# Seven-product block multiplication: products over four accumulator banks, batches in alternation, one result tile for two units

## The chip, the cores and the metric

One core of a Trainium2 chip runs the kernel. The metric is device time in microseconds (us) of one execution; three timed executions of the kernel before gave 1161.13, 1161.44 and 1161.69 us. TensorE is called PE, VectorE DVE, ScalarE ACT, GpSimd POOL, SyncE SP (it issues the DMAs).

## What is computed

Attention with a forgetting bias over 4 batches of 576 tokens, then two feed-forward layers on every token. The attention is as in the kernel's first third and is not touched. The layers are:

```python
h = x @ w_in                      # 2304x512 @ 512x2048
g = where(h >= 1, h, where(h <= -1, 0, (h + 1)**2 / 4))
x = g @ w_out                     # 2048x512
a = x @ w_a;  b = x @ w_b         # 512x1536 each
out = (a * b) @ w_out2            # 1536x512
```

## The kernel before

All data lies transposed: 128 features on the partitions, a batch's S = 576 tokens along the row. A *unit* is 128 features of a layer's hidden width: 16 in layer 1, 12 in layer 2. Each number is held as a high and a low part, and a product of two such numbers is three matmuls (`PASSES`, L953). A matmul here has 128 rows, 128 columns of weights and HN = 288 tokens (half a batch).

`ROUNDS` (L28) lists the work: batches 0 and 1 in the plain way, with attention of the other batches among it; then, from about 672 us, batches 2 and 3 through both layers by a seven-product scheme. For two units, the 2x2 block product (two halves of the features, two halves of the tokens) is made of seven products in place of eight. The sums of weight blocks are prepared by `load_set` (tiles `set`, three of them), those of the token blocks by `make_forms` (tiles `form`), once for a batch and layer.

`seven` (L1084) issues the seven products of one pair of units. Each is six matmuls, 288 columns wide. They accumulate in three places: X and Y, the two banks of a pair tile `pp`, and Z, one bank `ps`. The places take intermediate sums: a place is read out and then written on. The order of targets is X, Y, Z, X, Y, X, X (L1094). `gather` (L1123) reads after each of the first six: ACT copies products 0, 1 and 3 into a tile `tmp` (L1135), DVE adds products 2, 4 and 5 to it (L1137). The last X is read by the users: `h_seven` (L1145, relu, square, max/min in pieces of 576 and 288) or `ab_seven` (L1173, the product of a and b). `split_g` makes high and low parts into `g` tiles (L373, L1009). `y_step` (L1190) multiplies the `g` of a block of units by the second weights (matmuls L963) and adds the result to `y` (DVE, L1218; the first block is copied by ACT). In layer 1 a block is four units, in layer 2 two, and a block is finished for one batch before the other's begins.

PSUM has eight banks: two pairs `pp` and four single `ps`. A `product` takes a pair or two singles.

Nothing is placed by hand: each operation enters `Plan` (L140) with an engine, an estimated duration (`act`, `tt`, L272 to L277), a key (its wished time) and what it reads and writes. `Plan.run` then sets out, engine by engine, whatever can start first, and adds `LAT` (L143) after each operation. Each engine runs its list in that order, so the estimates decide the order of the instructions, not their time on the chip. `Banks.find` (L113) hands out PSUM, `Room.find` (L84) the SBUF places: `tmp_room` six tiles of 576 columns (three of them only in the second part), `g_room` seven.

Of the kernel before, what the change touches and what calls it, by code (L numbers as in the profile page):

```python
# [14 lines left out]
ALU = mybir.AluOpType  # L15
# [18 lines left out]
    (2, (2, 3), 0, 12, 2, True),  # L34
# [4 lines left out]

QK32 = 8  # L40
# [4 lines left out]
TMPS = 3  # L45
TMPS_LATE = 3
# [93 lines left out]
class Plan:  # L140


    LAT = {"PE": 0.3, "DVE": 0.2, "ACT": 0.15, "POOL": 0.5, "SP": 0.1}  # L143
# [128 lines left out]
def act(n):  # L272
    return 0.10 + 0.00083 * n


def tt(n):
    return 0.075 + 0.00104 * n  # L277
# [11 lines left out]
def tile_forgetting_attention_two_ffn(  # L289
# [92 lines left out]
    def dma(key, o, i, size, reads, writes, name, q=SP, issue=0.36, lat=2.0):  # L382
# [36 lines left out]
    tmp_room = plan.room(  # L419
        TMPS + TMPS_LATE,  # L420
        lambda k, ref: (const if k < TMPS else pool_of("sets")).tile([P, S], F32, tag=f"tmp{k}", name=f"tmp{k}", bufs=1),
        lambda k: k < TMPS or x_over(k),
    )
# [531 lines left out]
    def product(key, terms, hold, name):  # L955

        ps = bank(key, "either")
        for a in range(2):

            def mm(e, a=a):  # L960
                for k, (w, x, _) in enumerate(terms):
                    for t, (wu, xu) in enumerate(PASSES):
                        nc.tensor.matmul(  # L963
                            bank_of(ps, a)[:, :HN],
                            w(wu),
                            x(xu)[:, a * HN : (a + 1) * HN],
                            start=(k == 0 and t == 0),
                            stop=(k == len(terms) - 1 and t == len(PASSES) - 1),
                        )

            op({PE: 3 * len(terms) * HN * PE1}, key, mm, [r for t in terms for r in t[2]], [(ps, a)], hold=hold, name=name)
        return ps
# [111 lines left out]
    def seven(key, st, b, layer, hold, name, take):  # L1084

        xy, z = bank(key, "pair"), bank(key, "one")

        def at(n):
            return z.t[:, :HN] if n == 2 else xy.t[:, n, :HN]

        def mark(n):
            return (z, 0) if n == 2 else (xy, n)

        for n, (to, w, x, fresh) in enumerate((  # L1094
            (0, A11, B11, True),
            (1, S1, T1, True),
            (2, A12, B21, True),
            (0, S2, T2, False),
            (1, S4, B22, False),
            (0, S3, T3, False),  # L1100
            (0, A22, T4, False),
# [14 lines left out]
            kn = key + 1.6 * n  # L1116
            op({PE: 3 * NG2 * HN * PE1}, kn, mm, need, [mark(to)], hold=hold, name=name)
            take(n, kn - 6, lambda to=to: at(to), mark(to))
        return lambda: at(0), mark(0)

    HALF = (slice(0, HN), slice(HN, S))

    def gather(c):  # L1123

        def take(n, k, src, rd):
            what = {0: (0, 0), 1: (1, 1), 2: (0, 0), 3: (0, 1), 4: (0, 1), 5: (1, 1)}.get(n)
            if what is None:
                return
            f, a = what

            def part():
                return c[f].t[:, HALF[a]]

            if n in (0, 1, 3):
                op({ACT: act(HN)}, k, lambda e: nc.scalar.copy(part(), src()), [rd], [(c[f], a)], name="part")  # L1135
            else:
                op({DVE: tt(HN)}, k, lambda e: nc.vector.tensor_tensor(part(), src(), part(), op=ALU.add),  # L1137
                   [rd], [(c[f], a)], name="partadd")

        return take  # L1140

    def both(t):
        return [(t, 0), (t, 1)]

    def h_seven(key, st, b, g):  # L1145
# [5 lines left out]
        def relu(o, i):  # L1151
            return lambda e: nc.scalar.activation(o(), i(), AF.Relu, bias=0.5, scale=0.5)
# [4 lines left out]
        def at(r, sl):  # L1157
            return lambda: r.t[:, sl]
# [182 lines left out]
```

## Time and profile before

| | before |
|---|---|
| median of 3 runs | 1161.44 us |
| profiled execution, its own time | 1161.19 us |
| its span, first to last instruction | 1159.5 us |
| PE busy | 1078.6 us (93%), 8068 matmuls recorded |
| DVE busy | 734.3 us (63%) |
| ACT busy | 616.8 us (53%) |
| mean granted PE clock | 0.981 |

Busy time of PE counts overlapping matmuls once, with modelled ends; a stretch's matmul count times the distance between starts says more than its busy share. The chain of waits gives PE 74% of the span, ACT 12%, DVE 6%, DMA 5%. "L1106" is line 1106 of the kernel, `pp<-form,set` means a matmul that reads `form` and `set` and writes `pp`.

### The profile page before, as it was taken

What the parts mean: (1) busy time and instruction counts of PE and PEld (TensorE: products, weight loads), DVE (VectorE), ACT (ScalarE), POOL (GpSimd) and SP (SyncE); (2) the same over time, 40 slices, a digit from 0 to 9 for tenths busy, and PEclk for the clock granted to TensorE, in tenths of its full rate; (3) what the DMA queues carried; (4) which work ended last, traced back from release to release, by engine and by line L of the source; (5) the groups of instructions that cost most, each with busy time, mean ns of one, the idle gap of its engine ahead of it and who ended that gap; (6) DMA issues with size and microseconds to landing.
All of it is one profiled execution on the core that took longest, in us unless ns stands there. A gap on an engine that the chain in (4) does not pass through costs nothing.

```text
span 1159.5 us, 20668 instructions
## 1 busy us (share of the span) xinstructions
PE 1078.6 (93%) x8068; PEld 1011.9 (87%) x8068; DVE 734.3 (63%) x1463; ACT 616.8 (53%) x1381; POOL 40.2 (3%) x64
## 2 busy tenths in 40 slices
PE   9998987999999999899999888888888989999998
PEld 5777877998999999899999888888887978899898
DVE  7886673377687856668565574555556745665555
ACT  5986883466797767667653244544445333222211
POOL 2131210000000000000000000000000000000000
PEclk9998997999999999999999899999999899999999
DMA  5766786456475765655363571213131132222012
GB/s 182 229 190 168 178 172 175 153 197 160 171 192 163 198 146 183 165 153 207 91 160 116 174 262 37 108 38 106 41 99 48 38 109 73 96 87 73 3 36 82
DMA packets 84770, 152.35 MB, mean 131 GB/s; under 512 B 21320, under 2 KB 45896, under 8 KB 84672
## 3 DMA queue, kind: packets, MB, share of 16 engines
q1 hardware_dynamic: 84576, 150.88, 43.7%
q8 instruction: 63, 1.03, 0.4%
q14 instruction: 35, 0.29, 0.1%
q10 hardware_dynamic: 96, 0.15, 0.0%
HBM read 107.64 MB, written 42.79 MB: 130 GB/s over the span
## 4 chain that ended last, share of the span: by engine, by line
PE 74%; ACT 12%; DVE 6%; DMA 5%; issue 2%; SPq 0%; POOL 0%; DVEq 0%; ACTq 0%
PE pp L963 43%; PE pp L1106 16%; PE ps L750 3%; PE ps L700 2%; ACT tmp L1135 2%; DMA qkraw<-in_qk 2%; PE ps L1106 2%; PE ps L641 2%; DVE tmp L1137 2%; DMA conv<-in_w_in 2%; ACT p L675 2%; PE ps L963 1%; DMA conv<-in_w_out 1%; ACT pt L373 1%; PE ps L632 1%
## 5 line engine op out<-in xcount | busy, mean ns | idle before, releaser
L963 PE MATMUL pp<-g,whl 128*128 128x288 f32 x2574 | 359.3, 297 | 5.9 <-DVE y L1218 5.9
L963 PEld LDWEIGHTS pp<-g,whl 128*128 128x128 f32 x2574 | 348.7, 190 | 8.1 <-DVE y L1218 7.5
L963 PE MATMUL pp<-x,whl 128*128 128x288 f32 x1896 | 269.2, 298 | 4.5 <-ACT tmp L1017 2.5
L1106 PE MATMUL pp<-form,set 128*128 128x288 f32 x1440 | 227.3, 306 | 42.0 <-ACT tmp L1135 25.5
L963 PEld LDWEIGHTS pp<-x,whl 128*128 128x128 f32 x1896 | 255.9, 189 | 7.5 <-ACT tmp L1017 3.2
L1106 PEld LDWEIGHTS pp<-form,set 128*128 128x128 f32 x1440 | 201.6, 192 | 62.2 <-ACT tmp L1135 39.2
L1218 DVE TENSOR_TENSOR y<-pp,y 128x576 f32<-128x576 f32 x107 | 80.8, 755 | 78.8 <-PE pp L963 78.5
L1135 ACT COPY tmp<-pp 128x288 f32<-128x288 f32 x120 | 45.7, 399 | 140.6 <-PE pp L1106 140.6
L373 ACT CAST g<-tmp 128x576 fp32r<-128x576 f32 x106 | 71.3, 673 | 68.4 <-DVE tmp L1181 43.7
L1009 DVE TENSOR_TENSOR g<-tmp,g 128x576 fp32r<-128x576 f32 x112 | 84.7, 759 | 21.6 <-ACT g L373 20.8
L1137 DVE TENSOR_TENSOR tmp<-pp,tmp 128x288 f32<-128x288 f32 x80 | 35.1, 454 | 87.4 <-PE pp L1106 70.2
L675 ACT ACTIVATE p<-p,mx 112x576 f32<-112x576 f32 (+4 forms) x140 | 81.7, 585 | 7.6 <-DVE mx L660 7.0
L700 PE MATMUL ps<-ident,p 116*116 116x116 f32 (+2 forms) x420 | 65.0, 268 | 14.2 <-ACT p L675 12.1
L373 ACT COPY pt<-ps 116x448 f32<-116x448 f32 (+4 forms) x173 | 65.2, 399 | 18.0 <-PE ps L700 16.4
L926 ACT ACTIVATE conv<-conv 128x512 uint32<-128x512 uint32 x68 | 45.9, 675 | 43.4 <-DVE conv L936 21.3
L946 DVE TENSOR_TENSOR whl<-conv,whl 128x512 fp32r<-128x512 f32 x68 | 46.4, 687 | 32.6 <-ACT whl L373 32.4
L700 PEld LDWEIGHTS ps<-ident,p 116*116 116x116 f32 (+2 forms) x420 | 46.3, 136 | 23.5 <-ACT p L675 13.5
L750 PEld LDWEIGHTS ps<-pt,v 116*64 116x64 f32 (+1 forms) x832 | 52.4, 138 | 15.0 <-issue 6.1
L750 PE MATMUL ps<-pt,v 116*64 116x146 f32 (+5 forms) x832 | 63.8, 289 | 1.6 <-ACT pt L373 1.5
L660 DVE CUSTOM_DVE_ANT_0 p<-ps,hide 116x116 f32<-116x116 f32 (+1 forms) x112 | 49.6, 453 | 16.9 <-PE ps L641 15.6
L373 ACT CAST whl<-conv 128x512 fp32r<-128x512 f32 x57 | 34.8, 620 | 37.4 <-PE pp L963 37.2
L936 DVE CUSTOM_DVE_ANT_0 conv<-conv 128x1024 uint16<-128x1024 uint16 x68 | 46.9, 690 | 9.6 <-ACT conv L926 8.5
(100 smaller groups left out, 1137.8 us busy)
## 6 DMA issues: line engine op xcount, KB each, us to landing
whl<-keep_out SPq DMA_DIRECT2D x36, 512.0 KB
qkraw<-in_qk SPq DMA_DIRECT2D x112, 144.0 KB
conv<-in_w_out SPq DMA_DIRECT2D x28, 512.0 KB
keep_out<-whl SPq DMA_DIRECT2D x28, 512.0 KB
conv<-in_w_in SPq DMA_DIRECT2D x16, 512.0 KB
keep_in<-whl SPq DMA_DIRECT2D x16, 512.0 KB
conv<-in_w_a SPq DMA_DIRECT2D x12, 512.0 KB
conv<-in_w_b SPq DMA_DIRECT2D x12, 512.0 KB
```

The source lines that it names most:

```text
L373: nc.scalar.copy(o, i)
L660: nc.vector.tensor_tensor_reduce(out=psl(pref.t)[:r].rearrange("q (g n) -> q g n", g=parts), in0=pv()[:r, :parts, :w], in1=hide[:r, lag : ...
L675: nc.scalar.activation(p, p, AF.Exp, bias=mx.t[:r], scale=-1.0, accum_out=sm.t[:r, h % 2, i : i + 1])
L700: nc.tensor.transpose(pt.t[: rows[j], (j - j0) * QT : (j - j0) * QT + r], psl(pref.t)[:r, QT * j : QT * j + rows[j]], ident[:r, :r],)
L750: nc.tensor.matmul(ps.t[c0 : c0 + D, q0 - l : u - l], vt.t[: rows[j], j], pts[0].t[: rows[j], o + q0 : o + u], start=(j == 0), stop=(QT * ...
L936: op({DVE: tt(512)}, k, lambda e: vec.tensor_tensor(mu(), mu(), up(), op=ALU.add), [(we, 0)], [(wr, 0)], name="wadd", port=True)
L963: nc.tensor.matmul(bank_of(ps, a)[:, :HN], w(wu), x(xu)[:, a * HN : (a + 1) * HN], start=(k == 0 and t == 0), stop=(k == len(terms) - 1 an ...
L1009: op({DVE: tt(S)}, k, lambda e: nc.vector.tensor_tensor(g.t[:, 1], tmp.t, f32(g.t[:, 0]), op=ALU.subtract), [*need, (g, 0)], [(g, 1)], nam ...
L1106: nc.tensor.matmul(at(to), by_pair(st.t)[:, w, wu, g], forms[b, layer, g].t[:, x, xu], start=fresh and k == 0, stop=k == len(terms) - 1, s ...
L1135: op({ACT: act(HN)}, k, lambda e: nc.scalar.copy(part(), src()), [rd], [(c[f], a)], name="part")
L1137: op({DVE: tt(HN)}, k, lambda e: nc.vector.tensor_tensor(part(), src(), part(), op=ALU.add), [rd], [(c[f], a)], name="partadd")
L1218: nc.vector.tensor_tensor(o, i, o, op=ALU.add)
```

## The change

- `seven` takes a pair for Y and W, one bank for X and one for Z. The order of targets becomes Y, X, Z, W, Y, X, W. ACT copies Y (product 0) and X (product 1), 288 columns each; DVE adds Z (product 2) and W (product 3); after product 5 ACT copies X into two sections of the result at once (576 columns) and DVE adds X to a third; after product 6 one DVE operation of 576 columns adds Y and W.
- A pair's results lie in one tile `ct` of two rows of 576 (four such tiles); relu, square, max/min and the product of a and b take all 1152 columns in one instruction. `g_room` is left six places in the second part.
- A block's steps alternate: a pair of units for batch 2, the same for batch 3, the next pair for both; then y of four units for batch 2 and for batch 3, in layer 2 too. In y a product of four units is issued as two halves of two units.
- `Plan`'s estimates: `LAT` of PE 0.3 to 0.21, DVE 0.2 to 0.06, ACT 0.15 to 0.06; `act` 0.10 + 0.00083n to 0.15 + 0.00088n, `tt` 0.075 + 0.00104n to 0.15 + 0.00105n. They hold for the whole program, attention included.
- The forms of both batches for layer 1 are made ahead of the first seven products.

```diff
-    (2, (2, 3), 0, 12, 2, True),
+    (2, (2, 3), 0, 12, 4, True),
...
-    LAT = {"PE": 0.3, "DVE": 0.2, "ACT": 0.15, "POOL": 0.5, "SP": 0.1}
+    LAT = {"PE": 0.21, "DVE": 0.06, "ACT": 0.06, "POOL": 0.5, "SP": 0.1}
...
 def act(n):
-    return 0.10 + 0.00083 * n
+    return 0.15 + 0.00088 * n
 def tt(n):
-    return 0.075 + 0.00104 * n
+    return 0.15 + 0.00105 * n
...
-    def product(key, terms, hold, name):
+    def product(key, terms, hold, name, step=NC):
         ps = bank(key, "either")
-        for a in range(2):
+        for k0 in range(0, len(terms), step):
+            part = terms[k0 : k0 + step]
+            for a in range(2):
...
-    def seven(key, st, b, layer, hold, name, take):
-        xy, z = bank(key, "pair"), bank(key, "one")
+    def seven(key, st, b, layer, c, name):
+        yw, xb, zb = bank(key, "pair"), bank(key, "one"), bank(key, "one")
+        X, Z, Y, W = (xb, 0), (zb, 0), (yw, 0), (yw, 1)
...
-            (0, A11, B11, True),
-            (1, S1, T1, True),
-            (2, A12, B21, True),
-            (0, S2, T2, False),
-            (1, S4, B22, False),
-            (0, S3, T3, False),
-            (0, A22, T4, False),
+            (Y, S1, T1, True),
+            (X, A11, B11, True),
+            (Z, A12, B21, True),
+            (W, S3, T3, True),
+            (Y, S4, B22, False),
+            (X, S2, T2, False),
+            (W, A22, T4, False),
...
+            if n < 2:
+                m, j = ((Y, 3), (X, 0))[n]
+                op({ACT: act(HN)}, k, lambda e, m=m, n=n: nc.scalar.copy(cut(1 - n, 1 - n), at(m)), [m], [(c, j)], name="part")
+            elif n == 5:
+                op({ACT: act(S)}, k, lambda e: nc.scalar.copy(
+                    cut(0, 1, 2).rearrange("p (a n) -> p a n", a=2), at(X).unsqueeze(1).to_broadcast([P, 2, HN])),
+                   [X], [(c, 1), (c, 2)], name="part")
+            for m, f in {2: ((Z, 0),), 3: ((W, 1),), 5: ((X, 1),)}.get(n, ()):
+                op({DVE: tt(HN)}, k, lambda e, m=m, f=f: nc.vector.tensor_tensor(cut(f, f), at(m), cut(f, f), op=ALU.add),
+                   [m], [(c, 3 * f)], name="partadd")
+            if n == 6:
+                op({DVE: tt(S)}, k, lambda e: nc.vector.tensor_tensor(
+                    cut(0, 1, 2).rearrange("p (a n) -> p a n", a=2),
+                    yw.t[:, :, :HN],
+                    cut(0, 1, 2).rearrange("p (a n) -> p a n", a=2),
+                    op=ALU.add), [Y, W], [(c, 1), (c, 2)], name="partadd")
...
+        op({ACT: act(2 * S)}, k, lambda e: nc.scalar.activation(t.t, c.t, AF.Relu, bias=0.5, scale=0.5), got, [(t, 0)], name="relu")
+        op({ACT: act(2 * S)}, k, lambda e: nc.scalar.activation(t.t, t.t, AF.Square), (), [(t, 0)], name="square")
+        op({DVE: tt(2 * S)}, k, lambda e: nc.vector.scalar_tensor_tensor(t.t, c.t, 1.0, t.t, op0=ALU.max, op1=ALU.min),
+           got, [(t, 0)], name="max", port=True)
...
-        ps = product(key, terms, [y], "y")
+        ps = product(key, terms, [y], "y", 2 if (b, 1, 0) in forms else NC)
...
+            if strassen:
+                steps += [("g", layer, b, fs[n : n + 2], True) for n in range(0, len(fs), 2) for b in bs]
+                steps += [("y", layer, b, fs, True) for b in bs]
...
-                k = first[1, b] - 30 + 2 * g
+                k = first[1, 2] - 40 + 3 * (b - 2) + 2 * g
```

How the order moves, in the built programs (line numbers shift from L1106 to L1119 for the products of `seven`; a row is one or more instructions, `[waits ...]` names the engine or DMA queue whose semaphore the instruction waits for):

On PE before, the last five products of a pair of units in layer 1, batch 2 (`pp_79` is the pair that holds X and Y, `set_8422` the weights):

```order
L1106 MATMUL pp_79<-form_7391,set_8422 128x288 x3
L1106 MATMUL pp_79<-form_7451,set_8422 128x288 x3
L1106 MATMUL pp_79<-form_7391,set_8422 128x288 [waits DMAHW3_49,Activation_49]
L1106 MATMUL pp_79<-form_7391,set_8422 128x288 x2
L1106 MATMUL pp_79<-form_7451,set_8422 128x288 x3
L1106 MATMUL pp_79<-form_7391,set_8422 128x288 [waits Activation_49]
L1106 MATMUL pp_79<-form_7391,set_8422 128x288 x2
L1106 MATMUL pp_79<-form_7451,set_8422 128x288 x3
L1106 MATMUL pp_79<-form_7391,set_8422 128x288 [waits Activation_49]
L1106 MATMUL pp_79<-form_7391,set_8422 128x288 x2
L1106 MATMUL pp_79<-form_7451,set_8422 128x288 x3
L1106 MATMUL pp_79<-form_7391,set_8422 128x288 [waits DMAHW2_49,DVE_49]
```

Four of the five wait, each on a reader of the product just ahead, and all write one pair. In the changed program, the five last products of the same kind of pair (`pp_82` holds Y and W, `ps_83` X, `ps_84` Z):

```order
L1119 MATMUL ps_84<-form_7206,set_7536 128x288 x3
L1119 MATMUL ps_84<-form_7212,set_7536 128x288 x3
L1119 MATMUL pp_82<-form_7206,set_7536 128x288 [waits Activation_49]
L1119 MATMUL pp_82<-form_7206,set_7536 128x288 x2
L1119 MATMUL pp_82<-form_7212,set_7536 128x288 x3
L1119 MATMUL pp_82<-form_7206,set_7536 128x288 x3
L1119 MATMUL pp_82<-form_7212,set_7536 128x288 x3
L1119 MATMUL ps_83<-form_7206,set_7536 128x288 [waits DMAHW7_49,Activation_49]
L1119 MATMUL ps_83<-form_7206,set_7536 128x288 x2
L1119 MATMUL ps_83<-form_7212,set_7536 128x288 x3
L1119 MATMUL pp_82<-form_7206,set_7536 128x288 [waits DMAHW6_49,DVE_49]
L1119 MATMUL pp_82<-form_7206,set_7536 128x288 x2
```

Z, W, Y, X and W now follow in this order, and the waiting ones stand two or three products behind the one whose reader they wait for; W and Y stand side by side, on the two banks of one pair.

On DVE before, the additions of such a pair of units and what follows (`tmp` takes the sums, L1155 is max/min, L1009 the low part of `g`):

```order
L1137 TENSOR_TENSOR tmp_8414<-ps_81,tmp_8414 128x288 [waits Activation_49]
L1137 TENSOR_TENSOR tmp_8414<-pp_80,tmp_8414 128x288 [waits PE_49,Activation_49]
L1137 TENSOR_TENSOR tmp_8415<-pp_80,tmp_8415 128x288
L1155 SCALAR_TENSOR_TENSOR tmp_8550<-tmp_8414,tmp_8550 128x576 [waits DVE_49,Activation_49]
L1155 SCALAR_TENSOR_TENSOR tmp_8560<-tmp_8415,tmp_8560 128x288 [waits DVE_49,Activation_49]
L1009 TENSOR_TENSOR g_8584<-tmp_8550,g_8584 128x576 [waits Activation_49]
L1155 SCALAR_TENSOR_TENSOR tmp_8560<-pp_80,tmp_8560 128x288 [waits Activation_49]
```

and in the changed program, for two pairs of units in a row (`ct` takes the sums; L1140 the additions of 288 columns, L1143 that of 576, L1163 max/min of 1152 columns, L1153 the low part):

```order
L1140 TENSOR_TENSOR ct_8109<-ps_84,ct_8109 128x288 [waits PE_49,Activation_49]
L1140 TENSOR_TENSOR ct_8109<-pp_82,ct_8109 128x288 [waits PE_49]
L1140 TENSOR_TENSOR ct_8109<-ps_83,ct_8109 128x288 [waits DVE_49,Activation_49]
L1143 TENSOR_TENSOR ct_8109<-pp_82,ct_8109 128x576 [waits PE_49]
L1140 TENSOR_TENSOR ct_8163<-ps_84,ct_8163 128x288 [waits PE_49,Activation_49]
L1140 TENSOR_TENSOR ct_8163<-pp_81,ct_8163 128x288 [waits PE_49]
L1163 SCALAR_TENSOR_TENSOR ct_8178<-ct_8109,ct_8178 128x1152 [waits DVE_49,Activation_49]
L1140 TENSOR_TENSOR ct_8163<-ps_83,ct_8163 128x288 [waits DVE_49,Activation_49]
L1143 TENSOR_TENSOR ct_8163<-pp_81,ct_8163 128x576 [waits PE_49]
L1153 TENSOR_TENSOR g_8226<-ct_8178,g_8226 128x576 [waits Activation_49]
```

An operation of 1152 columns that belongs to the pair of units before now stands between the additions of W and of X of the next. The addition of X waits for an ACT instruction, too.

## Rows read from the trace of the kernel before

**Rows 1.** Busy time by stretch: engines, granted clock, DMA share.
```profile
core 0: us, PE busy (x) PEld busy (x) DVE busy (x) ACT busy (x) POOL busy (x), PEclk, DMA share, GB/s
0.00:640.00 640.00, 610.88 (x4790) 566.26 (x4791) 434.69 (x927) 434.25 (x1015) 40.18 (x64) 0.98 0.60 170
640.00:660.00 20.00, 14.73 (x96) 14.51 (x95) 9.07 (x15) 2.91 (x6) 0.00 (x0) 0.83 0.56 187
...
672.00:1155.00 483.00, 440.34 (x3092) 418.70 (x3091) 280.38 (x502) 174.16 (x351) 0.00 (x0) 0.99 0.22 76
```

**Rows 2.** What PE waited for, 672 to 1155 us: total, times, longest.
```profile
PE pp L1106 <- ACT tmp L1135: 25.5, 49, 2.8
PE pp L1106 <- DVE tmp L1137: 14.3, 27, 2.6
```

**Rows 3.** Timeline of PE, 658 to 670 us: start, duration, line, count, [idle before].
```profile
658.96 9.70 PE L963 MATMUL pp<-x,whl 128*128 128x288 f32 x72
668.50 1.74 PE L963 MATMUL ps<-x,whl 128*128 128x288 f32 x12
```

**Rows 4.** Timeline of PE in one group of seven products.
```profile
806.15 1.74 PE L1106 MATMUL pp<-form,set 128*128 128x288 f32 x12
808.38 1.07 PE L1106 MATMUL pp<-form,set 128*128 128x288 f32 x6 [0.49 <-ACT tmp L1135]
809.94 1.07 PE L1106 MATMUL pp<-form,set 128*128 128x288 f32 x6 [0.49 <-ACT tmp L1135]
811.50 1.06 PE L1106 MATMUL pp<-form,set 128*128 128x288 f32 x6 [0.49 <-ACT tmp L1135]
813.55 2.67 PE L1106 MATMUL pp<-form,set 128*128 128x288 f32 x18 [0.98 <-DVE tmp L1137]
```

**Rows 5.** Timeline of ACT in the same stretch.
```profile
807.93 0.40 ACT L1135 COPY tmp<-pp 128x288 f32<-128x288 f32 x1 [7.61 <-PE pp L1106]
809.49 0.40 ACT L1135 COPY tmp<-pp 128x288 f32<-128x288 f32 x1 [1.16 <-PE pp L1106]
811.05 0.40 ACT L1135 COPY tmp<-pp 128x288 f32<-128x288 f32 x1 [1.16 <-PE pp L1106]
```

**Rows 6.** Timeline of DVE in the same stretch.
```profile
812.67 0.82 DVE L1137 TENSOR_TENSOR tmp<-pp,tmp 128x288 f32<-128x288 f32 x2 [3.85 <-PE pp L1106]
```

**Rows 7.** Busy time in stretches of 20 us, those with a lower clock.
```profile
692.00:712.00 20.00, 16.75 (x110) 16.27 (x111) 14.22 (x27) 11.55 (x22) 0.00 (x0) 0.91 0.17 65
...
772.00:792.00 20.00, 17.06 (x108) 15.64 (x107) 9.07 (x16) 7.26 (x15) 0.00 (x0) 0.91 0.17 53
...
892.00:912.00 20.00, 15.53 (x92) 14.49 (x91) 15.91 (x30) 10.52 (x23) 0.00 (x0) 0.83 0.15 54
```

**Rows 8.** Groups by line, 672 to 1155 us: count | busy us, mean ns | idle.
```profile
L1218 DVE TENSOR_TENSOR y<-pp,y 128x576 f32<-128x576 f32 x62 | 46.8, 755 | 42.6 <-PE pp L963 42.4
L1135 ACT COPY tmp<-pp 128x288 f32<-128x288 f32 x120 | 45.7, 399 | 140.6 <-PE pp L1106 140.6
...
L1137 DVE TENSOR_TENSOR tmp<-pp,tmp 128x288 f32<-128x288 f32 x80 | 35.1, 454 | 87.4 <-PE pp L1106 70.2 <-ACT tmp L1135 17.1
...
L1053 DVE TENSOR_TENSOR set<-sums,set 128x1024 fp32r<-128x1024 f32 x19 | 23.2, 1220 | 5.4 <-ACT set L1052 5.4
...
L1052 ACT CAST set<-sums 128x1024 fp32r<-128x1024 f32 x19 | 19.9, 1049 | 34.4 <-DVE sums L1043 34.2
...
L1137 DVE TENSOR_TENSOR tmp<-ps,tmp 128x288 f32<-128x288 f32 x40 | 18.2, 454 | 33.1 <-ACT tmp L1135 24.1 <-PE ps L1106 8.7
...
L373 ACT COPY y<-pp 128x576 f32<-128x576 f32 x15 | 9.6, 639 | 20.4 <-PE pp L963 20.4
```

**Rows 9.** Timeline, 640 to 650 us.
```profile
640.31 1.27 SPq L385 DMA_DIRECT2D set<-keep_in  x3
...
646.39 1.22 DVE L1046 TENSOR_TENSOR sums<-set 128x1024 f32<-128x1024 f32 x1 [6.11 <-DMA set<-keep_in]
...
649.72 0.61 PE L963 MATMUL pp<-g,whl 128*128 128x288 f32 x1 [5.26 <-DVE y L1218]
```

More of the change, by code (lines that the diff above doesn't have):

```diff
@@ L37 @@
 POOL_UNTIL = 100
+PART = 0.8
 QK32 = 8
@@ L418, in tile_forgetting_attention_two_ffn, with ct_tile, ct_free @@
     x_over = gate_of("sets")
[L419 to L423, printed above, removed]
+    early = const.tile([P, 2, S], F32, tag="ct0", name="early", bufs=1)
+    third = pools["x"].tile([P, S], F32, name="third")
+    tmp_room = plan.room(3, lambda k, ref: early[:, k] if k < 2 else third)
+    users["x"].append(tmp_room)
+    g_room.gate = lambda k: k < G_BUFS - 1 or not x_over(k)
+    def ct_tile(k, ref):
+        home = pool_of("sets") if 0 < k < CTS else const
+        return home.tile([P, 2, S], F32, tag=f"ct{k}" if k < CTS else f"g{G_BUFS - 1}", name=f"ct{k}", bufs=1)
+    def ct_free(k):
+        last = g_room.places[-1]
+        return x_over(k) and (k < CTS or last is None or last.left == 0)
+    ct_room = plan.room(CTS + 1, ct_tile, ct_free)
     def set_tile(k, ref):
@@ L1115, in seven @@
             need = [(st, w)] + [(forms[b, layer, g], x if x < T1 else T1 + (x - T1) // 2 * 2) for g in range(NG2)]
[L1116 to L1140, printed above, removed]
@@ L1142, in both @@
-    def both(t):
-        return [(t, 0), (t, 1)]
-    def h_seven(key, st, b, g):
-        c = [Ref(tmp_room, key) for _ in range(2)]
-        t = [Ref(tmp_room, key + 2) for _ in range(2)]
-        src, rd = seven(key, st, b, 1, c, "h", gather(c))
-        k = key + 1
-        def relu(o, i):
-            return lambda e: nc.scalar.activation(o(), i(), AF.Relu, bias=0.5, scale=0.5)
-        def least(o, i):
-            return lambda e: nc.vector.scalar_tensor_tensor(o(), i(), 1.0, o(), op0=ALU.max, op1=ALU.min)
-        def at(r, sl):
-            return lambda: r.t[:, sl]
-        every = slice(0, S)
-        for f, sl, i, need, to in (
-            (0, every, at(c[0], every), both(c[0]), both(t[0])),
-            (1, HALF[1], at(c[1], HALF[1]), [(c[1], 1)], [(t[1], 1)]),
-            (1, HALF[0], src, [rd], [(t[1], 0)]),
-        ):
-            n, o = sl.stop - sl.start, at(t[f], sl)
-            op({ACT: act(n)}, k, relu(o, i), need, to, name="relu")
-            op({ACT: act(n)}, k, lambda e, o=o: nc.scalar.activation(o(), o(), AF.Square), (), to, name="square")
-            op({DVE: tt(n)}, k, least(o, i), need, to, name="max")
-        for f in range(2):
-            split_g(k, g[f], t[f], both(t[f]))
@@ L1173, in ab_seven @@
[L1173 to L1188 removed]
+            kn = key + PART * n
@@ new lines, in tile_forgetting_attention_two_ffn @@
+        ks = []
+        for w in names:
+            key = T0 + per * spent
+            spent += cost(kind, layer, len(fs), strassen) / layer
+            ks.append(key)
+            if (w, fs[0], bunch) not in hls:
+                hls[w, fs[0], bunch] = (load_set if strassen else load_unit)(w, fs[0], key)
+        ws = [hls[w, fs[0], bunch] for w in names]
+        g = [Ref(g_room, ks[0] + (3 if strassen else 0.0)) for _ in fs]
+        gs.update({(layer, b, f): r for f, r in zip(fs, g)})
+        if strassen:
+            (h_seven if layer == 1 else ab_seven)(*ks, *ws, b, g)
+        else:
+            (h_step if layer == 1 else ab_step)(*ks, *ws, b, g[0])
```

128 lines of the change are left out of this document (57 added, 71 removed).

## Prediction

> **What bounds the kernel now.** I read the busy time by stretch first, to find where PE is not full. Attention and the plain layers take the first 640 us, and there PE is busy 610.9 us [rows 1]. From 672 us to 1155 us the seven-product scheme for batches 2 and 3 runs, and only this part's instructions are rewritten. In it PE is busy 440.3 of 483 us, DVE 280.4 and ACT 174.2, and DMA has a share of 0.22 [rows 1]. So PE sets the pace, and something keeps it waiting.
>
> The timeline of PE gives the price of a matmul that does not wait: 72 of them start between 658.96 and 668.50 us, 9.54 us, or 0.1325 us each [rows 3]. The stretch from 672 us holds 3096 in the built program (the trace records 3092 [rows 1]). At 0.1325 us that is 410.2 us. The stretch takes 483, so **73 us** are lost there. That is the pool from which this change can take.
>
> What it consists of: the list of waits gives PE 25.5 us behind the copies of line 1135 and 14.3 us behind the additions of line 1137 [rows 2]. The timeline of one group of seven shows how. After two products (twelve matmuls) three follow at 808.38, 809.94 and 811.50, 1.56 us apart, while six matmuls are worth 0.795 us [rows 4]. So one such wait costs 0.765 us, of which the view counts 0.49; the rest is the emptying and refilling of PE. ACT's rows show the partner: each copy starts 0.04 us after the product before it ends, takes 0.40 us, and the next product starts 0.05 us after it [rows 4, 5]. The first copy starts at 807.93, after both products: the two banks of a pair are waited for as one. Then two additions of DVE, 0.82 us together, hold back the last product until 813.55 [rows 4, 6]. PE, ACT and DVE take turns instead of working side by side. The clock adds its part: in the three stretches of 20 us with a granted clock of 0.91, 0.91 and 0.83 [rows 7], 20 x (0.09 + 0.09 + 0.17) = 7 us of PE work are lost.
>
> **The change, part by part.**
>
> *Waits within the seven.* For each product of the two built programs that waits on ACT or DVE, I counted the matmuls on PE between the last one that the reader waits for and the waiting one. Before, 43 waits on a copy of line 1135 and 8 on an addition of line 1137 have none between: 51 x 0.765 = 39 us. In the changed program 11 and 3 are left: 14 x 0.765 = 10.7 us. Gain: **28 us**.
>
> *Waits that have cover.* The rest of the 73 us, 73 - 39 - 7 = 27 us, comes from waits with one or more products between, where the reader was late. Before, 33 of these waits have one product of cover (0.795 us), 38 have two. In the changed program 24 have one, 46 two and 49 three. I scale the 27 us by the short ones, 24/33: 20 us, a gain of **7 us**. Bounds: none of it lost (a gain of 27), or twice as much as now (a loss of 27), since all reads now have a tighter partner, below.
>
> The cover must be held against the work. For the second W, one product lies between, 0.795 us; its addition takes 0.454 us [rows 8] where the copy took 0.40, so it needs 0.82 us from the end of the one product to the start of the other: cover but for 0.03 us, if DVE is free. For X two products lie between, 1.59 us, but two engines read it: ACT copies 576 columns (0.639 us, the row of the copy to `y` [rows 8]), DVE adds 288 (0.454). Before, no place is read by two engines after one product; in the changed order the addition waits for ACT. In turn, with the same gaps, that is 0.765 + 0.24 + 0.50 = 1.51 us, 0.08 us short of the cover. The Trainium skill (PSUM — Partial Sum Buffer, on bank collisions) says that two engines must not touch one bank at once, two reads included; no run here shows it. Read side by side, the two would need 1.0 us, and I would put the covered waits at 10 us in place of 20; the sum stays with 20.
>
> *Engine work.* DVE: before, 120 additions of 288 columns, 53.3 us [rows 8]; now as many plus 40 of 576 at 0.755 us: +31 us. Blocks of four units in layer 2 take away 24 of the additions to `y` (64 to 40), at 0.755 us [rows 8]: -18 us. One instruction of 1152 columns in place of two or three saves fixed time only; from 576 and 1024 columns (0.755 and 1.220 us [rows 8]) it takes 1.35 us. DVE thus does up to 294 us in this part, some 66% of a shorter stretch. ACT: 120 copies, 45.7 us, become 80 of 0.40 and 40 of 0.64, +12 us on 174; relu and square on 1152 columns take 1.16 us (0.639 and, for 1024, 1.049 [rows 8]) and save starts. Neither engine becomes the bound by its sum. All this lies beside PE; it counts only where it makes a reader late, and that is in the 20 us.
>
> *Clock.* Long waits go with the low clock (0.83 in the worst 20 us). With half of the waiting gone I keep 3 of 7 us: **4 us** gained; bounds 0 to 7.
>
> *Start of the part.* The first `set`'s sums were set on DVE ahead of an addition to `y`; DVE waited 6.11 us for their DMA, and PE 5.26 us for that addition, with the clock at 0.83 over 20 us [rows 1, 9]: 5.3 + 3.4 = 8.7 us. In the changed order these sums stand 12 matmuls ahead of the first seven (180 before), and that addition no longer stands behind them. But the loads of the forms of both batches and their subtractions now stand earlier, and they too wait for DMAs, with additions to `y` behind them; and the first group must wait for its sums. I take **4 us** of gain less 2 us for the first group; bounds: 8.7 gained, 8 lost. Batch 3's forms no longer fall among the first groups; what that gives is part of the 7 us of covered waits.
>
> *The first part.* The new estimates reorder attention and the plain layers; no instruction is added there. PE loses 29 us to waits and has a clock of 0.98 [rows 1]. These can move either way: 0, bounds 10 gained and 10 lost.
>
> *SP and POOL* get no new work: each set and each second weight is still loaded once for both batches. The second `set` of a pair in layer 2 has 72 matmuls (9.5 us) from issue to first use; DVE's wait for such a load was 6.11 us [rows 9], so it is covered. `g_room` with six places for eight `g` of a block makes batch 3's second pair wait until y of batch 2 frees places, with 24 matmuls (3.2 us) between the freeing and the use of the new `g`; two high and two low parts one after the other fit (four operations of at most 0.755 us, partly side by side): nothing, unless DVE is late.
>
> **The sum.** 28 + 7 + 4 + 4 - 2 = 41 us off the profiled execution's 1161.2 us, whose span is 1159.5 us (it stands 0.25 us below the median): **1120 us**, 3.5% less.
>
> **The rivals.**
>
> *DVE late, half the gain.* Additions of W and X have 0 to 0.08 us to spare, and an operation of 1.35 us of the other pair now stands between them in DVE's order. If each of the 80 reads is late by 0.25 us more on average, 20 us come back: **1140 us**. For it: DVE's share within the groups (outside y) is far above 66%. Against: the order puts the long operations where gaps were estimated.
>
> *DVE late at every read, slower.* The same mechanism at its full price: with the long operation just begun, a read comes up to 1.35 us late. The part without any lateness loses 10.7 + 3 + 2 = 16 us; from a mean of (73 - 16)/80 = 0.71 us on, the change costs time. At 1.0 us it loses 96 us in place of 73: **1184 us**. For it: the plan does not know that the two banks of a pair are waited for as one, nor that X's two reads go in turn, so its estimates are too early at both places. Against: before, all waits behind DVE make 14.3 us [rows 2].
>
> *No change.* The pair still joins Y and W, and if products on it take turns with the readers as before, nothing is won: 1161 us. Against: the count above.
>
> *All of it.* Covered waits vanish, as they would with DVE on time: 27 us in place of 7, **1100 us**.
>
> **How the numbers follow.** The forecast's own case (1105 to 1133 us) gets 0.56, half the gain (1133 to 1158) 0.22, almost all (below 1105) 0.12, no change 0.04, slower 0.06. A difference of 0.2% (2.3 us) is about what a measurement can tell from none. So faster 0.90, same 0.04, slower 0.06. The range leaves out slower, no change and the ends of two other cases, about 0.2: 1100 to 1148 us.
>
> **What would show it.** Right: in the rewritten part waits of PE behind copies fall below 10 us (25.5 now), the copies start while PE runs another place's product, the stretch takes some 440 us for 3096 matmuls. The wait that is left stands behind DVE additions. Wrong: waits behind DVE above 30 us, or a new wait on a DMA or on `ct` and `g` places, or a first part that is more than 10 us longer.

## The result and the profile after

The changed kernel takes **1084.7 us** (median of 4 runs, 1081.83 to 1085.86) against 1161.57 us for the kernel before on the same chip: ratio 0.9325, 95% interval 0.9291 to 0.9358. The forecast was 1120 us with a range of 1100 to 1148: the direction was right, but the gain of 77 us is almost twice the 41 us forecast, and the time lies below the range.

The profiled execution of the changed kernel took 1084.1 us, its span is 1082.4. Its busy time by stretch, in the columns of [rows 1]; the first product of seven starts at 653.4 us (671.7 before):

```profile
core 0: us, PE busy (x) PEld busy (x) DVE busy (x) ACT busy (x) POOL busy (x), PEclk, DMA share, GB/s
100.00:250.00 150.00, 141.63 (x1126) 134.23 (x1125) 95.95 (x201) 105.56 (x247) 12.39 (x18) 0.97 0.69 195
640.00:653.40 13.40, 13.40 (x103) 13.40 (x102) 12.11 (x25) 6.46 (x13) 0.00 (x0) 1.00 0.58 208
653.40:1078.00 424.60, 416.91 (x3096) 412.34 (x3095) 276.68 (x452) 166.08 (x267) 0.00 (x0) 1.00 0.25 85
```

The same 150 us of the kernel before, and its stretch from the first product of seven on:

```profile
100.00:250.00 150.00, 132.57 (x1046) 124.96 (x1043) 86.25 (x180) 98.55 (x235) 13.61 (x16) 0.93 0.65 176
...
671.68:1155.10 483.42, 440.76 (x3096) 419.12 (x3095) 280.50 (x502) 174.16 (x351) 0.00 (x0) 0.99 0.22 77
```

So the 77.1 us of span fall into two: the rewritten part went from 483.4 to 424.6 us (-58.8; 410.2 is its matmuls without any wait), the first part from 671.7 to 653.4 us (-18.3).

What PE waited for in the rewritten part after, against [rows 2]:

```profile
PE pp L1119 <- ACT ct L1134: 5.4, 11, 0.5
PE pp L1119 <- DVE ct L1140: 2.0, 4, 0.6
PE pp L1119 <- DVE set L1065: 0.2, 1, 0.2
```

76 waits behind copies and additions have become 15. The timeline of PE, DVE and ACT in one place of the changed kernel (start, duration, ..., count, [idle before <- releaser]) shows both a wait that is left and the reads that no longer hold PE:

```profile
725.47 0.96 PE L1119 MATMUL pp<-form,set 128*128 128x288 f32 x6
726.46 0.40 ACT L1134 COPY ct<-pp 128x288 f32<-128x288 f32 x1 [0.77 <-PE pp L1119]
...
726.91 1.06 PE L1119 MATMUL pp<-form,set 128*128 128x288 f32 x6 [0.49 <-ACT ct L1134]
...
728.46 1.35 DVE L1163 SCALAR_TENSOR_TENSOR ct<-ct,ct 128x1152 f32<-128x1152 f32 x1
...
730.49 0.46 DVE L1140 TENSOR_TENSOR ct<-ps,ct 128x288 f32<-128x288 f32 x1 [0.31 <-PE ps L1119]
...
731.00 0.63 ACT L1136 COPY ct<-ps 128x576 f32<-128x576 f32 x1
731.09 1.76 PE L1119 MATMUL ps<-form,set 128*128 128x288 f32 x12
...
732.69 1.76 PE L1119 MATMUL pp<-form,set 128*128 128x288 f32 x12
```

At 725.47 and 726.91 two products on one pair follow each other: 1.44 us apart in place of 0.795, the old turn with ACT. At 730.49 DVE reads X and at 731.00 ACT reads it after DVE has ended, while PE goes on: its next twelve matmuls take 1.60 us, 0.133 each.

A better account than the view's waits comes from the starts: for every stretch of matmuls, the distance to the next start less 0.1325 us for each matmul is lost, and goes to the wait named there. Added up over the rewritten part, all 3096 matmuls (the sums stand some 0.3 us above 73.2 and 14.4, since the last matmuls end 0.5 us after the part's end as taken here):

| us lost (waits) | before | after |
|---|---|---|
| behind copies of ACT | 36.7 (49) | 7.5 (11) |
| behind additions of DVE | 22.1 (27) | 3.0 (4) |
| behind forms, sets, y | 3.3 (4) | 0.4 (1) |
| no wait named (low clock, small gaps) | 11.5 | 3.7 |

The new instructions cost what the prediction set, in groups by line of the rewritten part (against [rows 8]; count | busy us, mean ns | idle before):

```profile
L1143 DVE TENSOR_TENSOR ct<-pp,ct 128x576 f32<-128x576 f32 x40 | 30.0, 751 | 3.9 <-PE pp L1119 3.6
...
L1136 ACT COPY ct<-ps 128x576 f32<-128x576 f32 x40 | 25.6, 639 | 61.5 <-PE ps L1119 58.1 <-DVE ct L1140 3.4
...
L1163 DVE SCALAR_TENSOR_TENSOR ct<-ct,ct 128x1152 f32<-128x1152 f32 x16 | 21.6, 1350 | 0.0
```

DVE is busy 276.7 of 424.6 us (65%), ACT 166.1; neither bounds the part.

### The profile page after: what moved, and what is told of

Same layout as the page of the kernel before. It is cut to its first block, busy times and chain, and to the rows that moved or that the text cites. A ratio compares the mean times of both kernels' runs of the same rounds, so it can differ in the third digit from the quotient of the medians.

```text
span 1082.4 us, 20564 instructions
## 1 busy us (share of the span) xinstructions
PE 1051.3 (97%) x8068; PEld 1004.6 (93%) x8068; DVE 740.1 (68%) x1430; ACT 612.0 (57%) x1304; POOL 36.5 (3%) x65
## 4 chain that ended last, share of the span: by engine, by line
PE 88%; DMA 5%; DVE 2%; ACT 2%; issue 1%; SPq 1%; POOL 0%; DVEq 0%; ACTq 0%; POOLq 0%
PE pp L975 49%; PE pp L1119 12%; PE ps L1119 8%; PE ps L760 5%; PE ps L710 4%; PE ps L975 4%; PE ps L651 2%; DMA conv<-in_w_b 2%; PE ps L642 1%; PE pp L651 1%; DMA conv<-in_w_in 1%; DMA keep_out<-whl 1%; PE pp L642 1%; SPq L385 1%; DMA keep_in<-whl 1%
## 5 line engine op out<-in xcount | busy, mean ns | idle before, releaser
L975 PE MATMUL pp<-g,whl 128*128 128x288 f32 x2394 | 331.3, 297 | 5.8 <-ACT whl L373 5.0
L975 PEld LDWEIGHTS pp<-g,whl 128*128 128x128 f32 x2394 | 322.5, 189 | 7.8 <-ACT whl L373 5.2
L1119 PE MATMUL pp<-form,set 128*128 128x288 f32 x960 | 147.4, 298 | 7.7 <-ACT ct L1134 5.4
L1119 PEld LDWEIGHTS pp<-form,set 128*128 128x128 f32 x960 | 132.5, 188 | 12.1 <-ACT ct L1134 8.3
L1119 PE MATMUL ps<-form,set 128*128 128x288 f32 x720 | 109.0, 296 | 0.0
L1119 PEld LDWEIGHTS ps<-form,set 128*128 128x128 f32 x720 | 100.1, 188 | 0.0
L1140 DVE TENSOR_TENSOR ct<-ps,ct 128x288 f32<-128x288 f32 x80 | 36.4, 455 | 54.2 <-PE ps L1119 34.7
L373 ACT COPY pt<-ps 112x112 f32<-112x112 f32 (+4 forms) x172 | 63.7, 392 | 15.7 <-PE ps L710 14.0
L956 DVE TENSOR_TENSOR whl<-conv,whl 128x512 fp32r<-128x512 f32 x68 | 46.5, 690 | 22.6 <-ACT whl L373 22.3
L1136 ACT COPY ct<-ps 128x576 f32<-128x576 f32 x40 | 25.6, 639 | 61.5 <-PE ps L1119 58.1
L1152 ACT CAST g<-ct 128x576 fp32r<-128x576 f32 x56 | 35.0, 673 | 40.7 <-PE pp L975 23.0
```

The lines of the kernel that those rows point to most:

```text
L373: nc.scalar.copy(o, i)
L956: op({DVE: tt(512)}, k + 1, lambda e: vec.tensor_tensor(half(1), value(), f32(half(0)), op=ALU.subtract), [(wr, 0), (hl, 0)], [(hl, 1)], n ...
L975: nc.tensor.matmul(bank_of(ps, a)[:, :HN], w(wu), x(xu)[:, a * HN : (a + 1) * HN], start=(k == 0 and t == 0), stop=(k == len(terms) - 1 an ...
L1119: nc.tensor.matmul(at(to), by_pair(st.t)[:, w, wu, g], forms[b, layer, g].t[:, x, xu], start=fresh and k == 0, stop=k == len(terms) - 1, s ...
L1140: op({DVE: tt(HN)}, k, lambda e, m=m, f=f: nc.vector.tensor_tensor(cut(f, f), at(m), cut(f, f), op=ALU.add), [m], [(c, 3 * f)], name="part ...
L1152: op({ACT: act(S)}, k, lambda e, f=f: nc.scalar.copy(g[f].t[:, 0], t.t[:, f]), need, [(g[f], 0)], name="ghi")
```

## The experiments

Questions: what of the change gave the 58.8 us of the rewritten part, and what the 18.3 us of the first. All results in one table; "first" is the start of the first product of seven, "part" from there to 4.4 us before the span's end, both of the profiled execution; the ratio is to the kernel before on the same chip. e1 to e4 shared one chip, e5, e6, e7 and e9 another, e8, e10 and e11 a third; the changed kernel and e12 ran apart. The median of the kernel before differed by 4 us among them, so times across these groups are compared by ratios, or by their parts.

| run | median us | ratio, 95% interval | first | part |
|---|---|---|---|---|
| before | 1157.6 to 1161.6 | 1 | 671.7 | 483.4 |
| changed | 1084.7 | 0.9325 (0.9291 to 0.9358) | 653.4 | 424.6 |
| e1_estimates_only | 1146.2 | 0.9894 (0.9875 to 0.9912) | 658.1 | 483.1 |
| e2_old_estimates | 1086.1 | 0.9382 (0.9368 to 0.9396) | 660.8 | 419.1 |
| e3b_batch_two | 1087.6 | 0.9397 (0.9378 to 0.9417) | 649.3 | 430.6 |
| e4_pair_known | 1068.9 | 0.9235 (0.9220 to 0.9251) | 647.9 | 413.6 |
| e5_max_twice | 1094.2 | 0.9448 (0.9434 to 0.9463) | 650.8 | 436.7 |
| e6_before_pair_known | 1144.7 | 0.9896 (0.9865 to 0.9926) | 670.5 | 470.1 |
| e7_steps_only | 1139.3 | 0.9846 (0.9822 to 0.9870) | 660.0 | 477.5 |
| e8_lat_only | 1175.0 | 1.0150 (1.0088 to 1.0211) | 681.3 | 491.9 |
| e9_sums_later | 1151.8 | 0.9948 (0.9929 to 0.9967) | 664.3 | 483.5 |
| e10_three_singles | 1109.1 | 0.9589 (0.9569 to 0.9609) | 669.0 | 433.6 |
| e11_act_tt_only | 1140.0 | 0.9858 (0.9832 to 0.9883) | 660.6 | 477.0 |
| e12_singles_and_steps | 1091.5 | 0.9422 (0.9403 to 0.9440) | 659.4 | 425.2 |

### e1, e2: the estimates alone, and all but the estimates

e1 is the kernel before with the new `LAT`, `act` and `tt`; e2 the changed kernel with the old ones:

```diff
-    LAT = {"PE": 0.3, "DVE": 0.2, "ACT": 0.15, "POOL": 0.5, "SP": 0.1}
+    LAT = {"PE": 0.21, "DVE": 0.06, "ACT": 0.06, "POOL": 0.5, "SP": 0.1}
...
-    return 0.10 + 0.00083 * n
+    return 0.15 + 0.00088 * n
...
-    return 0.075 + 0.00104 * n
+    return 0.15 + 0.00105 * n
```

> The kernel before with only the plan's estimates of the change (LAT, act, tt). The rewritten part is the stretch from the first of the seven products on (483 us before, 425 after); the first part is all ahead of it (672 us before, 653 after). Theory A, the places of the products make the gain of the rewritten part, the estimates that of the first part: first part 653 us +-5, rewritten part 478 to 486 us, PE waits behind copies of line 1135 again about 25 us; 1143 us in all. Theory B, the closer estimates make both: rewritten part 455 to 465 us, some 1118 us in all. Theory C, the first part moves by chance with any new order: first part anywhere from 660 to 685 us.

> The changed kernel with the estimates of before. Theory A (places for the rewritten part, estimates for the first): first part back at 672 us +-5, rewritten part 424 to 430 us, 1103 us in all. Theory B (estimates for both): rewritten part 440 to 455 us since readers are planned too early or too late, 1120 us in all. Theory C (any new order moves the first part): first part 655 to 668 us.

In the old structure the estimates leave the rewritten part as it was (483.1 for 483.4 us) and shorten the first part by 13.6 us. In the new structure they shorten the first part by 7.4 us and lengthen the rewritten one by 5.5, which leaves 2 us of span (1084.3 for 1082.4) and 0.6% between the ratios: nearly all of the change's gain is there without them. Theory A was right for e1 but for some 5 us of the first part; in e2 the first part came out as theory C had it, and the rewritten part shorter than any theory had it. The largest difference in the first part is one wait. With the old estimates, e2's list of PE's waits up to 640 us begins

```profile
PE ps L710 <- ACT p L685: 11.4, 4, 9.5
PE ps L651 <- ACT xraw L373: 5.2, 1, 5.2
```

and with the new ones that of the changed kernel

```profile
PE pp L975 <- ACT whl L373: 5.0, 1, 5.0
PE pp L975 <- ACT early L1029: 2.7, 1, 2.7
PE ps L651 <- ACT xraw L373: 2.2, 1, 2.2
```

The kernel before waits 12.1 us behind that same ACT operation on `p`, 10.1 us of it at once. That this wait alone makes the gain is not shown: other waits come in its place, and e8, below, has only 2.9 us of it and a longer first part.

### e8, e11: which of the estimates

The same two halves of that edit, each alone in the kernel before.

> The kernel before with the new LAT alone (act and tt old). All new estimates in the kernel before took 12 us (1158.4 to 1146.2), all in the first part, where 100 to 250 us loses its 10.1 us wait behind ACT. If LAT is what moves that instruction: 1146 us, PE busy 141 to 142 of the 150 us from 100 us on. If act and tt are: no change, 1156 to 1160 us, 133 of 150. The rewritten part stays at 480 to 486 us in both.

> The kernel before with the new act and tt alone (LAT old). The mirror of the run before: if LAT moves the late instruction, no change here, 1156 to 1160 us and 133 of 150 us; if act and tt do, 1146 us and 141 to 142 of 150. If both show the gain, any small shift of the estimates leaves the bad order of before, which then was chance. The built program has 32 and 7 waits without cover in place of 43 and 8: by 0.765 us each the rewritten part would fall by 9 us to 474 us.

Neither expectation for e8 held: `LAT` alone makes the kernel slower by 17 us (its four times lie between 1165.6 and 1181.8, and the profiled one took 1179.3), `act` and `tt` alone faster by 18, both together faster by 12. They don't add. Nor did e11 go as forecast: PE is busy 136.9 of the 150 us from 100 us on, between the two numbers, and its first part has a new wait of 9.1 us. No rule of "better estimates" is shown by this; a shift of about a tenth of a microsecond in the planner throws another order, and its worth in the first part ran from 9.6 us lost (e8) to 13.6 gained (e1).

### e9: the stall at 640 us

The prediction read the stall [rows 9] as DVE waiting for the first set's load with an addition to `y` behind it. e9 is the kernel before, where the planner's latency for that one load is longer:

```diff
-                P * 2048 * n, [("kept", name, at_f)], [(st, j) for j in range(j0, j0 + n)], "set")
+                P * 2048 * n, [("kept", name, at_f)], [(st, j) for j in range(j0, j0 + n)], "set", lat=2.0 if f or name != "in" else 11.0)
```

> The kernel before, where the plan is told that the loads of the first set land 9 us later; DVE then has that set's sums behind the addition to y and the first forms, and nothing else moves in the built program but some 25 rows of DVE. Theory (the stall at 640 us is DVE waiting for that load with the addition behind it): 5.3 us of PE's wait and up to 3.4 us of low clock go, the first part falls from 671.7 to about 663 to 666 us, the time by 6 to 9 us. Rival (PE would have waited for something else there): the first part falls by less than 2 us.

The first part falls by 7.4 us, the time by 0.52%, and the waits of the rewritten part stay the same to the tenth:

```profile
640.00:664.31 24.31, 24.31 (x185) 24.31 (x185) 18.40 (x34) 8.43 (x16) 0.00 (x0) 1.00 0.77 252
```

```profile
PE pp L1106 <- ACT tmp L1135: 25.5, 49, 2.8
PE pp L1106 <- DVE tmp L1137: 14.3, 27, 2.6
```

PE is full and at full clock where before it had 14.73 of 20 us at 0.83 [rows 1]. That cause is shown: 7.4 us for a load believed to land earlier than it does.

### e7, e3b: the order of steps

e7 gives the kernel before the new steps alone (pairs of both batches in turn, y of four units in layer 2 too, forms early); e3b gives the changed kernel the old steps, with blocks of two units in layer 2 (blocks of four, batch by batch, were not run); this is e3b's edit of the steps:

```diff
-                steps += [("g", layer, b, fs[n : n + 2], True) for n in range(0, len(fs), 2) for b in bs]
-                steps += [("y", layer, b, fs, True) for b in bs]
+                for b in bs:
+                    steps += [("g", layer, b, fs[n : n + 2], True) for n in range(0, len(fs), 2)]
+                    steps.append(("y", layer, b, fs, True))
```

> The kernel before with the changed kernel's order of steps alone: pairs of both batches in turn, then y of four units in both layers, the forms early; old targets X Y Z X Y X X, old results in pieces, old estimates. Built, 40 waits on ACT and 9 on DVE have no product between: 49 x 0.765 = 37 us. Theory 1 (the targets and places made the covered waits vanish): the rewritten part stays at 470 to 485 us, the first part falls to about 661 (as with the old estimates in the changed kernel), in all 1135 to 1150 us. Rival (taking the batches in turn is what hid the covered waits, some 24 us): the part takes 410 + 37 + 5 = about 452 us, in all 1115 to 1122 us.

> The changed kernel with the order of steps of before: batch 2's block, then batch 3's, blocks of two units in layer 2; places, result tile and estimates as changed. Theory A (the places alone): rewritten part 425 to 431 us, total within 8 us of the changed kernel. Theory D (the alternation of batches and the long y give the readers their cover): rewritten part 440 us or more, total over 1100 us, PE waits behind copies and additions above 20 us (7.6 us after).

e7: the steps alone take 11.7 us from the first part (e9's 7.4 is in it) and 6 from the rewritten one, whose waits stay; the rival's 452 us is out:

```profile
PE pp L1106 <- ACT tmp L1135: 21.8, 46, 0.9
PE pp L1106 <- DVE tmp L1137: 9.9, 19, 1.0
PE pp L1106 <- ACT tmp L1176: 4.0, 3, 1.3
```

e3b came out as theory A had it: without the turns of batches only 5 waits behind copies and additions are left (3.8 us by starts), and y waits for its last `g` instead; the part is 6 us longer, the time 0.3% longer by the medians, 0.8% by the ratios:

```profile
PE pp L975 <- DVE g L1153: 5.0, 6, 2.0
PE pp L975 <- ACT g L1152: 3.2, 1, 3.2
```

So taking the batches in turn hides the way to `g`; it isn't what removed the waits on copies and additions. Without the new order of steps, the rest of the change gives 52.8 of the 58.8 us (483.4 to 430.6); its new targets and its result tile were not run apart.

### e10, e12: no pair in the seven

e10 is the kernel before with X, Y and Z in three single banks; targets, reads, steps and estimates are old. e12 adds the new steps.

```diff
-        xy, z = bank(key, "pair"), bank(key, "one")
+        places = [bank(key, "one") for _ in range(3)]
...
-            return z.t[:, :HN] if n == 2 else xy.t[:, n, :HN]
+            return places[n].t[:, :HN]
...
-            return (z, 0) if n == 2 else (xy, n)
+            return (places[n], 0)
```

> The kernel before, where X, Y and Z are three single banks; targets X Y Z X Y X X, steps, estimates, results in pieces as they were. A bank is then waited for alone: in the built program no copy and 10 additions (product 5, whose bank product 6 takes at once) have no product between before the next use, 51 before. Theory (the pair, waited for as one, is what made the turns, and with them the late readers): 10 x 0.765 = 8 us, 4 to 12 us for late additions and 10 us of clock and gaps as before: the rewritten part takes 432 to 442 us (483 before), in all 1107 to 1118 us. Rival (the new targets are needed, since five of seven products still go to two places): the part stays above 455 us, in all over 1130 us.

> The kernel before with two parts: three single banks for X, Y, Z, and the changed kernel's order of steps; old targets, old reads in pieces, old estimates. Built, 12 additions (product 5 to 6) have no product between, no copy has. With the three single banks alone the rewritten part took 433.6 us, of it 19 us behind 10 such additions, two of them 7.7 and 3.1 us. Theory (the pair and the steps carry nearly all; targets and whole-row results only remove the last turns): 12 x 1.05 us = 13 us and some 5 us of others: a part of 424 to 431 us, a first part of about 660 (as with the steps alone), in all 1088 to 1096 us, 3 to 11 us over the changed kernel. Rival (the new targets are worth more once the batches take turns): a part above 440 us, in all over 1103 us.

Both came out as expected by the theory (e12's first part was within 1 us of it). e10 alone takes 49.8 of the 58.8 us: 433.6 us. Its waits:

```profile
PE ps L1106 <- DVE tmp L1137: 14.8, 10, 7.6
PE pp L963 <- ACT g L373: 0.6, 1, 0.6
PE ps L1106 <- ACT tmp L1135: 0.6, 1, 0.6
```

and its timeline, where the same copies, of the same length, now run beside 42 matmuls in a row:

```profile
818.24 5.75 PE L1106 MATMUL ps<-form,set 128*128 128x288 f32 x42
...
819.23 0.40 ACT L1135 COPY tmp<-ps 128x288 f32<-128x288 f32 x1 [10.85 <-PE ps L1106]
820.02 0.40 ACT L1135 COPY tmp<-ps 128x288 f32<-128x288 f32 x1 [0.39 <-PE ps L1106]
...
821.70 0.46 DVE L1137 TENSOR_TENSOR tmp<-ps,tmp 128x288 f32<-128x288 f32 x1 [2.50 <-PE ps L1106]
...
823.30 0.46 DVE L1137 TENSOR_TENSOR tmp<-ps,tmp 128x288 f32<-128x288 f32 x1 [0.78 <-PE ps L1106]
```

The copies stand 0.79 us apart, one product; the additions one by one, where [rows 6] had two in a row without idle time between (19 times in the part before, 3 times two or three in e10, 4 times after the change). With the steps too (e12) the part is 425.2 us, that of the changed kernel. But e12 has the old estimates, and so has e2, where the part is 419.1 us: at the same estimates and steps the new targets and whole-row results are 6 us better in this part, 0.4% by the ratios, though they keep a pair.

e10 frees the pair tiles for `y` as well; that this is no part of its gain was not tried apart. Directly it can't be much: in the part before, PE lost 1.1 us (3 waits) behind additions to `y`.

### e4, e6: the planner told that a pair is one

In the changed kernel the two products of a pair that were planned side by side are waited for together. e4 tells the plan so, by the marks of what is written and read; nothing else changes. e6 does the same in the kernel before (one line, `mark`).

```diff
-            op({PE: 3 * NG2 * HN * PE1}, kn, mm, need, [to], hold=[c, yw], name=name)
+            op({PE: 3 * NG2 * HN * PE1}, kn, mm, need, [(to[0], 0)], hold=[c, yw], name=name)
```

(and `[m]` and `[Y, W]` of the reads in the same way)

> The changed kernel, with the plan told that the two banks of the pair (Y and W) are waited for as one: the 14 waits with no product between are gone from the order. If these waits are what is left of the loss (14 x 0.765 = 10.7 us of 14.5): PE waits behind copies below 2 us, rewritten part 414 to 418 us, total 7 to 11 us less than the changed kernel. Rival: the stricter order makes other readers late, rewritten part 423 us or more, no gain.

> The kernel before, where only the plan learns that X and Y, the banks of one pair, are waited for as one. In the built program 37 waits on copies and 11 on additions have no product between, 48 in place of 51. Theory (four places are needed; knowing alone does not help where five of seven products go to one pair): the rewritten part takes 475 to 490 us (483 before), the time stays within 10 us of the kernel before. Rival (the plan only lacked the knowledge): a gain as when the changed kernel's plan was told, 11 us or more in the part, below 472.

e4 is the fastest version: 1068.9 us, and its ratio lies below the changed kernel's interval: it beats both kernels. Of the 16.5 us of span against the changed kernel 11.0 lie in the rewritten part; the other 5.5 lie in the first, where only the order moved. In its rewritten part, 3.4 us above the least, one wait is left:

```profile
647.90:1061.50 413.60, 413.00 (x3095) 411.67 (x3095) 279.76 (x455) 165.97 (x270) 0.00 (x0) 1.00 0.26 88
```

```profile
PE pp L1119 <- DVE ct L1140: 0.2, 1, 0.2
```

For e6 my theory fell, and the rival's number came out: the part is 470.1 us, 13 less than before, where I had expected 475 to 490 and the rival less than 472. So the knowledge was worth about as much in either kernel. The count of waits without a product between (48 for 51) does not tell that gain. By starts, 6.8 of it lie behind copies (29.9 us, 38 waits), 4.1 behind additions (18.0 us, 11 waits). Still, 60 us over the least remain: with five of seven products on one pair, the planner found no order without turns.

### e5: how much lateness of DVE is free

The changed kernel with max/min of layer 1 issued twice, unknown to the plan.

```diff
-        op({DVE: tt(2 * S)}, k, lambda e: nc.vector.scalar_tensor_tensor(t.t, c.t, 1.0, t.t, op0=ALU.max, op1=ALU.min),
-           got, [(t, 0)], name="max", port=True)
+        def least(e):
+            for _ in range(2):
+                nc.vector.scalar_tensor_tensor(t.t, c.t, 1.0, t.t, op0=ALU.max, op1=ALU.min)
+        op({DVE: tt(2 * S)}, k, least, got, [(t, 0)], name="max", port=True)
```

> The changed kernel, with max/min of 1152 columns issued twice in layer 1 (the second does the same again, the plan does not know of it): 16 times 1.35 us more on DVE, between the additions that read X and W. Theory (the reads have room): an addition has one to three products of six matmuls before its bank is written again, 0.8 to 2.4 us, and takes 0.46 us, so most of the 16 delays are swallowed: 0 to 6 us over the changed kernel, 1085 to 1091 us. Rival (as the prediction put it, 0 to 0.08 us to spare): each delay reaches PE nearly whole, 16 x (1.35 - 0.08) = 20 us, 1100 to 1107 us, with waits of PE behind DVE up by over 12 us.

Between the two: the rewritten part is 12.1 us longer, the ratio 1.3% higher (the medians stand 9.5 us apart). New are

```profile
PE ps L1119 <- DVE ct L1140: 4.6, 6, 1.2
PE pp L975 <- DVE ct L1143: 3.5, 5, 0.9
```

Both parts hold the same 3096 matmuls, so the loss grew by those 12.1 us (14.7 to 26.8 by starts), 12.1 / 16 = 0.76 us for each 1.35 us put in. So somewhat less than half of such a delay is swallowed: on average the reads have room for some 0.6 us.

## Why the prediction was wrong in size

**Waits within the seven: right.** Forecast 39 us before, 10.7 left, 14 waits at 0.765. Measured after: 10.5 us in 15 waits (7.5 + 3.0), 0.70 each. The 39 us are a count times a price; in the trace before, 40 copies that started as the product just ahead ended cost 29.3 us (0.73 each), and 8 additions that followed another addition ([rows 6] is one of them) 12.0 (1.5 each). By the price these 48 would be 36.7 us; so some 5 us of the term below are turns, priced too low. That the wait left would stand behind DVE additions did not come out: 11 of the 15 stand behind copies.

**Waits that have cover: the step that failed.** "I scale the 27 us by the short ones, 24/33: 20 us." By starts, before, 73.5 - 39 - 11.5 leaves 23.0 us; after, 14.6 - 10.5 - 3.7 leaves 0.4. So this term gave 22.6 us in place of 7. It was left at some 20 us too much because its premise was wrong: I took lateness as a thing that goes with the number of waits with one product of cover. In e10's built program 25 waits on copies and additions still have one product between (33 before), and all that PE lost behind copies there is 0.8 us. Behind additions it lost 19.1 us in 10 waits, and 10 additions there have no product between. What makes readers late is then the pair. In part it is this: two reads that the pair holds back together run one after the other, 0.82 us [rows 6] where a product gives 0.795 us. In the trace before, 15 of the 76 waits stand behind such a second read (8 additions, 12.0 us; 7 copies, 5.9 us). Besides these and the 40 copies above, 21 waits (11.6 us) have other late readers, 10 of them additions that stood behind a product of a and b (L1181), as here in the kernel before:

```profile
1052.14 0.76 DVE L1181 TENSOR_TENSOR tmp<-tmp,tmp 128x576 f32<-128x576 f32 x1
1052.82 0.45 DVE L1137 TENSOR_TENSOR tmp<-pp,tmp 128x288 f32<-128x288 f32 x1
...
1053.33 1.06 PE L1106 MATMUL pp<-form,set 128*128 128x288 f32 x6 [0.18 <-DVE tmp L1137]
```

Without the pair they went as well (e10); why these did is not shown one by one. So most of both terms, 39 and 27 us, had one cause: without the pair (e10) the part loses 23 us in place of 73. I had the rows for it ([rows 4, 6]: "waited for as one", two additions in a row) and split it into two terms, of which only one could gain.

The side question of X's readers had no weight. The trace shows the two reads in turn (730.49, then 731.00 after the first had ended), as forecast, and PE did not wait. The Trainium skill (PSUM — Partial Sum Buffer, on bank collisions) says that two engines must not touch one bank at once; the trace agrees in so far as in none of the 40 cases did the copy of X overlap the addition of that X, and no run tries it. Neither 20 us nor 10 was right.

**Clock: right in kind.** 4 of 7 us were forecast; the mean granted clock of the part is 1.00, and the loss without a named wait, small gaps included, fell by 7.8, from 11.5 to 3.7 us.

**Start and first part: the other step that failed.** Forecast 2 us and 0, with bounds of 8.7 and 10 us of gain; measured 18.3, close to both bounds together. These 16 us count as much in the miss as the 16 us of the covered waits. The stall's reading was right (e9: 7.4 us of the 8.7), but I took off half for new waits that did not come: in the changed kernel PE is full from 640 us on. The estimates gave 7.4 us more (e2 against the changed kernel). The 0 was a choice between signs, and the sign could not be read off the trace before: e8 and e11 give either. That the estimates brought a gain here, and not a loss, was luck.

**The sum with measured terms:** 28.5 (10.5 left of 39) + 22.6 + 7.8 + 18.3 = 77.2 us for 77.1 in the span. As the first two were split by the count and not by the trace, only their sum is measured.

**The rivals.** DVE's lateness (1140 and 1184 us): waits behind DVE are 2.0 us, far below the 30 us that would have shown it. Its mechanism exists (e5), but on average some 0.6 us of each delay is free, not "0 to 0.08 us". "All of it" (1100 us) was the right case for the rewritten part, where the covered waits are gone; what it lacked is the first part. That case, below 1105 us, had been given a chance of 0.12.

## What to carry to other kernels

When an accumulator tile spans two banks, ask what releases it: here one wait for both banks turned a copy of 0.40 us into a loss of some 0.7 us on PE and made the second reader late as well. Three single banks, a change of three lines, gave 50 of the 59 us; telling the planner what is really waited for gave the changed kernel another 11 in that part, and the kernel before 13.

When lost time is split into terms, look whether one row explains two of them: then they go together. And judge a planner's estimates by a run of each alone: two halves of one edit were worth +17 and -18 us by the orders that they happened to give.

## What was not expected

- Two edits of the estimates, -17.6 us (`act`, `tt`) and +17.4 us (`LAT`) by themselves, give -12 us together.
- The same first part's instructions in the same order started the first product of seven at 653.4 us in the changed kernel and at 650.8 in e5, on another chip: a difference of 2.6 us that no change explains, so a difference of that size between two first parts tells nothing.
- 1.35 us more on DVE, sixteen times, costs PE 0.76 us each time on average, in a part where DVE is busy 65% without them.
